# A linear-attention and bilinear-FFN kernel: shorter zero products at the start, two second-weight products side by side, one slot's transposes and loads ahead of a store

## The chip, the cores and the metric

The kernel runs on one core of a Trainium2 chip. The metric is the device time of one execution in microseconds (us). The engines are TensorE (PE for its products, PEld for its weight loads), VectorE (DVE), ScalarE (ACT), GpSimd (POOL) and SyncE (SP), which issues nearly all DMAs. The five engines run side by side and wait for each other on semaphores.

## The reference

There are two steps. The first is a linear attention with a decaying state, over 4 batches, 8 heads, 768 positions and a head size of 64; the second is a bilinear feed-forward layer on its result, laid out as 3072 tokens by 512.

```python
gamma = 1.0 - 2.0 ** (-5.0 - np.arange(H))
for t in range(S):
    state = gamma * state + einsum('bhd,bhe->bhde', k[:, :, t], v[:, :, t])
    y[:, :, t] = scale * einsum('bhd,bhde->bhe', q[:, :, t], state)
x = y.transpose(0, 2, 1, 3).reshape(3072, 512)
out = ((x @ w_a) * (x @ w_b)) @ w_out        # w_a, w_b: 512 x 1536; w_out: 1536 x 512
```

## The kernel before

**Attention.** The 3072 tokens are cut into 24 slots of 128 positions (six in each batch). The decay is folded into k and q by tables (`scaled`, L285, writes both into one bf16 tile `kqb`), so that a slot needs: the transposes of its k and q (`kqT`), the scores inside the slot (`at`, L338 and L452), a mask on DVE (`aT`), the product with the running state (`inter`), the product with v (`intra`), the update of the state (`update`), and a copy of the result to `xt`. The first six slots are taken as three pairs by functions whose names end in 2 (`casts2`, `flip2`, `scores2`, `update2`, `intra2`, `inter2`, `leave2`); `flip2` transposes on TensorE. From slot 6 on, `casts` makes `kqb` on POOL, `flip` (L311) has SP issue one DMA transpose of it, and `casts(t)` ends with the loads of slot t+2. `turn(new, old)` then does the TensorE part of a slot pair.

**Feed-forward.** `xt` is consumed in seven groups of slots (`TILES`, group J). For each of twelve column blocks ft of the weights, `ffn_a(J, ft)` (L533) makes four products that add up to a, and ACT copies them to `asb`; `ffn_g(J, ft)` (L545) makes four products with the second weight, and DVE multiplies them by `asb` into `ht` (L547). For group 0 the first two blocks are taken in two halves of the tokens: columns 0 to W2 belong to the first slot pair, W2 to 2*W2 to the second. The last product is done by `ffn_out` for group 0, and for the others by a seven-product scheme (`Group`, `Unit`, `single`). A PSUM bank for a or g comes from a ring of three (`psff`): the oldest idle bank is taken, and it is given back in program order.

**Weights.** They arrive as f32 by DMA into `wst` tiles and are cast to bf16 on POOL (`cast_w`, L244). `cast_w(0, parts=2)` makes four casts: the first weight's blocks 0 and 1 (`wa_bf`), then the second weight's blocks 0 and 1 (`wb_bf`).

**Order.** Everything is written out by hand in one program order, and `seq` chains the instructions of each engine in that order. SP is one queue: loads, DMA transposes and stores leave it in the order in which the program reaches them. A finished output tile is not stored at once: it goes to `held`, and `store()` (L559) issues what is held at the next `ffn_out(.., 0)` or `ffn_ab`.

**Zero products.** `warm(pool, tag, *cols)` (L514 to L519) gives TensorE products of a zero tile that nobody reads. The tile `zero` is f32, and in the trace each such f32 product is two TensorE instructions. There are five calls ahead of the first weights: after them in order stand the transposes of k (pair 0), those of q, the scores and the first state update, and, for pair 1, the scores. The last call takes a bank of the ring `psff` and gives it back.

**Around slot 9.** The program order there is: `ffn_out(0, 2, 0)`, which stores tile 1 of the output; `ffn_out(0, 2, 1)`; `turn(6, None, V_)`; the sums of `ht` on DVE; `ffn_out(0, 3, 0)`, which stores tile 2; `ffn_out(0, 3, 1)`; `casts(9)`; `turn(None, 6)`; `single(1, ..)`, which stores tile 3; `casts(10)`; `casts(11)`; and, after more blocks, `turn(8, None)` and `turn(10, 8)`. The scores of slot 11 are the first TensorE work of `turn(10, 8)`.

Of the kernel before, what the change touches and what calls it, by code (L numbers as in the profile page):

```python
# [29 lines left out]
def kernel(  # L30
# [10 lines left out]
    nc = tc.nc  # L41
    P = 128
    B, H, S, D = q.shape
    NCH = S // P
    HP = H // 2
# [25 lines left out]
    psat = ctx.enter_context(tc.tile_pool(name="psat", bufs=1, space=bass.MemoryType.PSUM))  # L71
# [23 lines left out]
    psff = Ring()  # L95
# [4 lines left out]
    def seq(bi):  # L100
        ins = bi.ins
        prev = last.get(ins.engine)
        if prev is not None:
            tc.add_manual_dep(ins, prev.name, nosync, reason="program order")
        last[ins.engine] = ins
        return bi
# [4 lines left out]
    def load_slot(t, names="kqv"):  # L111
        b, ci = divmod(t, NCH)
        for nm in names:
            src = {"k": k, "q": q, "v": v}[nm]
            if nm == "q":
                if t % 2 == 0:
                    load_two(nm, src, b, ci // 2, t)
                continue
            if t % 2 == 0:
                whole[nm] = raw.tile([P, 2, H, D], F32, tag=nm + "f", name=nm + "f")  # L120
            raws[nm, t] = whole[nm][:, t % 2]
            s = src[b, :, ci * P : (ci + 1) * P, :].rearrange("h p d -> p h d")
            seq(nc.sync.dma_start(out=raws[nm, t], in_=s))
# [5 lines left out]
    def load_two(nm, src, b, u, t):  # L129
        f = raw.tile([P, H, 2, D], F32, tag=nm + "f", name=nm + "f")  # L130
        s = src[b, :, 2 * u * P : 2 * (u + 1) * P, :].rearrange("h (p two) d -> p h two d", two=2)
        seq(nc.sync.dma_start(out=f, in_=s))  # L132
        for par in range(2):
            raws[nm, t + par] = f[:, :, par, :]
# [5 lines left out]
    def load_wide(nm, n):  # L140
        src = {"a": moe_w_a, "b": moe_w_b}[nm]
        for i in range(2):
            st = wstage.tile([P, 2, 2 * WC], F32, tag="w", name="wst" + nm)
            s = src[2 * i * P : 2 * (i + 1) * P, 2 * n * WC : 2 * (n + 1) * WC]
            seq(nc.sync.dma_start(out=st, in_=s.rearrange("(c p) f -> p c f", p=P)))
            wst[nm, n, i] = st
# [16 lines left out]
    def issue_loads(n):  # L163
        for _ in range(min(n, len(pending))):
            what = pending.pop(0)
            n = int(what[1:])
            if what[0] in "ab":
                load_wide(what[0], n)
            elif what[0] in "kqv":
                load_two(what[0], {"k": k, "q": q, "v": v}[what[0]], 0, n, 2 * n)  # L170
            else:
                {"p": load_pair, "s": load_slots, "t": load_slot, "w": load_w, "o": load_o}[what[0]](n)
# [5 lines left out]
    zero = osbp.tile([P, DM], F32, tag="osb", name="zero")  # L178
# [6 lines left out]
    ident = const.tile([P, P], BF16, name="ident")  # L185
# [20 lines left out]
    gbd = [const.tile([P, HP, P], BF16, name=f"gbd{i}") for i in range(2)]  # L206
# [33 lines left out]
    def cast(engine, dst, src):  # L240
        if engine is nc.scalar:
            seq(nc.scalar.copy(dst, src))
        else:
            seq(engine.tensor_copy(dst, src))  # L244
# [29 lines left out]
    def scaled(eng, t, i):  # L274
        tab = tabs[0] if i else tabs[1 if t < 2 * PAIRS else 2]
        dst, src, tab = kqb[t][:, i], raws["kq"[i], t], tab[:, t % NCH]
        if t < 2 * PAIRS:
            dst, src = (x.rearrange("p (hp r) d -> p hp r d", r=2) if x is src else x
                        for x in (dst, src))
            tab = tab.rearrange("p (hp r) o -> p hp r o", r=2).to_broadcast([P, HP, 2, D])  # L280
        else:
            dst = dst.rearrange("p hp r d -> p r hp d")
            src = src.rearrange("p (r hp) d -> p r hp d", r=2)
            tab = tab.rearrange("p (r hp) o -> p r hp o", r=2).to_broadcast([P, 2, HP, D])
        seq(eng.tensor_tensor(dst, src, tab, op=ALU.mult))  # L285

    def new_nat(t):
        kqb[t] = nat.tile([P, 2, HP, 2, D], BF16, tag="kqb", name="kqb")
        kb[t], qb[t] = kqb[t][:, 0], kqb[t][:, 1]
        vb[t] = nat.tile([P, H, D], BF16, tag="vb", name="vb")  # L290

    def casts(t):
        new_nat(t)
        scaled(nc.gpsimd, t, 0)
        scaled(nc.gpsimd, t, 1)
        if t not in range(12, 20):
            cast(nc.gpsimd, vb[t], raws["v", t])
        flip(t)
        u = t + 2
        if u in V_LATE:  # L300
            load_slot(u, "kq")
            if u % 2:
                load_slot(u - 1, "v")
                load_slot(u, "v")
        elif u < NSLOT:
            load_slot(u)

    def flip(t):
        if t % 2 == 0:
            kqT[t // 2] = tra.tile([P, 2, 2, HP, P], BF16, tag="kqT", name="kqT", bufs=3)  # L310
        seq(nc.sync.dma_start_transpose(  # L311
            out=kqT[t // 2][:, t % 2].rearrange("p a b c -> p (a b) c"),
            in_=kqb[t].rearrange("p a hp r d -> p (a hp r d)")))
# [195 lines left out]
    def xcols(J, kt, c0, c1):  # L509
        if J < 2:  # L510
            return xt[J][:, c0 // P : c1 // P, kt, :]
        return xt[J][:, kt, c0:c1]

    def warm(pool, tag, *cols):  # L514
        idle = pool.tile([P, HP * P], F32, tag=tag, name="idle")
        for n in cols:
            seq(nc.tensor.matmul(idle[:, :n], zero[:, :P], zero[:, :n], start=True, stop=True,
                                 skip_group_check=True))
        psff.back(idle)  # L519

# [18 lines left out]
    def ffn_g(J, ft, c0=0, c1=None):  # L539
        c1 = TILES[J] * P if c1 is None else c1  # L540
        fs = slice(ft * P, (ft + 1) * P)
        bank = psff.tile([P, 4 * P], F32, tag="ff", name="g")
        g = bank[:, : c1 - c0]
        for kt in range(KT):
            seq(nc.tensor.matmul(g, wb_bf[:, kt, fs], xcols(J, kt, c0, c1),  # L545
                                 start=(kt == 0), stop=(kt == KT - 1)))
        seq(nc.vector.tensor_tensor(ht[J][:, ft, c0:c1], g, asbs.pop((J, ft, c0)), op=ALU.mult))  # L547
        psff.back(bank)
# [8 lines left out]
    def store():  # L557
        for dst, src in held:
            seq(nc.sync.dma_start(out=dst, in_=src))  # L559
        held.clear()  # L560
# [3 lines left out]
    def ffn_out(J, i, n):  # L564
        if n == 0:
            store()
            plain_out[i] = psff.tile([P, DM], F32, tag="ff", name="o")
        o = plain_out[i]
        for ft in range(NP * n, NP * n + NP):
            seq(nc.tensor.matmul(o, ht[J][:, ft, i * P : (i + 1) * P], wo_bf[:, ft],  # L570
                                 start=(ft == 0), stop=(ft == NFT - 1), skip_group_check=True))
        if n:
            osb = osbp.tile([P, DM], F32, tag="osb", name="osb")
            cast(nc.scalar, osb, o)
            psff.back(o)
            held.append((rows(J, i // 2, i % 2), osb))

    def rows(J, u, r):
        n0 = (sum(TILES[:J]) + 2 * u) * P
        return out[n0 : n0 + 2 * P, :].rearrange("(n r) d -> r n d", r=2)[r]  # L580
# [36 lines left out]
    def hsums(J, a, b, eng):  # L617
        for s in (2, 1, 4):
            hsum(J, s, a, b, eng)
# [257 lines left out]

    D_, G_, A_ = nc.vector, nc.gpsimd, nc.scalar
    K, Q = 0, 1
    warm(psat, "y1", 512, 512, 256)  # L880
    casts2(0, {(K, 1): D_, (K, 0): D_, (Q, 1): D_, (Q, 0): D_})
    flip2(0, K, [((0, 1), A_)])
    warm(psat, "y1", 128)
    flip2(0, Q, [((1,), D_)])
    flip2(0, Q, [((0,), D_)])
    warm(psat, "y1", 256)
    scores2(0, 1)
    scores2(0, 0, "ff")
    update2(0, 0)
    warm(psat, "y1", 512)  # L890
    casts2(1, {(K, 0): G_, (K, 1): G_, (Q, 1): D_, (Q, 0): D_})
    update2(0, 1)
    intra2(0, 1, True)
# [2 lines left out]
    flip2(1, K, [((0, 1), A_)])  # L896
    leave2(0, (A_, A_))
    flip2(1, Q, [((1,), D_), ((0,), D_)])
    warm(psff, "ff", 256)
    scores2(1, 0, "ff")  # L900
    scores2(1, 1)
    update2(1, 0)
# [1 line left out]
    W2 = 2 * P  # L904
# [5 lines left out]
    leave2(1, (A_, D_))  # L910
    update2(1, 1)
    ffn_g(0, 0, 0, W2)
    issue_loads(100)
    cast_w(1, parts=2)
    ffn_a(0, 0, W2, 2 * W2)
    ffn_a(0, 1, W2, 2 * W2)
    ffn_g(0, 1, 0, W2)
    ffn_g(0, 0, W2, 2 * W2)
    ffn_g(0, 1, W2, 2 * W2)
    cast_wide("a", 1)  # L920
# [62 lines left out]
    turn(6, None, V_)  # L983
    hsum(1, 3, 0, 6)
    hsums(1, 0, 6, V_)
    ffn_out(0, 3, 0)
    ffn_out(0, 3, 1)
    casts(9)
    turn(None, 6)
    single(1, AT0, AT1, FF)  # L990
    casts(10)
# [100 lines left out]
```

## Time and profile before

| | |
|---|---|
| time, median of 3 runs | 219.66 us (219.35 to 219.67) |
| the profiled execution | 219.63 us |
| its span, first to last instruction | 217.9 us |
| TensorE busy | 211.4 us, 97% of the span |
| VectorE, ScalarE, GpSimd busy | 65%, 46%, 68% |
| granted TensorE clock over the span | 1.000 |
| read from and written to HBM | 28.31 MB and 6.29 MB |

The profiled execution's own time, its span and what lies around it, is 0.03 us under the median of the runs. In the profile a line "start, us, engine, line, operation, out<-in, xcount" is a run of like instructions: when the first began and how long it was until the last ended. "SPq" is the time in which SP issued a DMA. "[0.29 <-POOL wb_bf L244]" says how long the engine sat idle just before, and what it waited for.

### The profile page before, as it was taken

How to read it: one execution, taken by the hardware profiler on the slowest of the kernel's cores; microseconds unless marked ns; L12 is line 12 of the kernel's file. 1: busy time of each engine (PE TensorE's matmuls, PEld its weight loads, DVE VectorE, ACT ScalarE, POOL GpSimd, SP SyncE). 2: the span in 40 equal slices, each digit the busy share in tenths (PEclk: the TensorE clock that was granted, in tenths of full speed). 3: DMA queues.
4: the chain of work that ended last, by engine and by line, in shares of the span. 5: the costliest groups of instructions: out<-in, count | busy, mean ns of one | idle time of the engine just before them, and what ended most of it. 6: DMA issues, size and time to landing. Idle time of an engine off the chain costs nothing.

```text
span 217.9 us, 5672 instructions
## 1 busy us (share of the span) xinstructions
PE 211.4 (97%) x2244; PEld 143.6 (66%) x2244; DVE 141.5 (65%) x258; ACT 100.8 (46%) x221; POOL 147.9 (68%) x172
## 2 busy tenths in 40 slices
PE   7889999999999999999999999999999999999994
PEld 3557445587458888888888665456864444458883
DVE  3776446845873486355477245896687797688962
ACT  3256335343224444455576344455546656652331
POOL 5265876779344578579856948899999999960000
PEclk9999999999999999999999999999999999999999
DMA  6999999999999999999999996990022000000055
GB/s 163 290 321 365 384 303 361 384 263 236 181 239 257 196 231 214 195 232 245 196 202 272 207 193 173 237 150 3 5 86 106 0 2 3 0 2 0 27 193 169
DMA packets 85146, 39.68 MB, mean 182 GB/s; under 512 B 57472, under 2 KB 78848, under 8 KB 85120
## 3 DMA queue, kind: packets, MB, share of 16 engines
q1 hardware_dynamic: 84976, 39.26, 80.7%
q8 instruction: 17, 0.28, 0.6%
q14 instruction: 9, 0.07, 0.1%
q10 hardware_dynamic: 144, 0.07, 0.1%
HBM read 28.31 MB, written 6.29 MB: 159 GB/s over the span
## 4 chain that ended last, share of the span: by engine, by line
PE 84%; SPq 7%; DMA 6%; issue 1%; POOL 0%; ACT 0%; DVE 0%; ACTq 0%
PE g L545 17%; PE a L533 17%; PE mA L650 11%; PE uA L801 10%; PE mB L650 6%; PE uB L801 5%; PE o L570 5%; SPq L132 4%; DMA wstb<-in_moe_w_b_dram 4%; PE mC L650 3%; DMA kqT<-kqb 2%; PE uC L801 2%; PE at L338 2%; PE y L386 2%; PE st L356 1%; PE y L376 1%
## 5 line engine op out<-in xcount | busy, mean ns | idle before, releaser
L547 DVE TENSOR_TENSOR ht<-g,asb 128x256 bf16<-128x256 f32 (+1 forms) x74 | 37.2, 503 | 37.5 <-PE g L545 34.5
L545 PE MATMUL g<-xt,wb_bf 128*128 128x256 bf16 (+1 forms) x296 | 52.5, 304 | 0.3 <-POOL wb_bf L244 0.3
L533 PE MATMUL a<-xt,wa_bf 128*128 128x256 bf16 (+1 forms) x296 | 52.7, 304 | 0.1
L536 ACT CAST asb<-a 128x256 bf16<-128x256 f32 (+1 forms) x74 | 32.3, 437 | 39.2 <-PE a L533 37.7
L545 PEld LDWEIGHTS <-wb_bf 128*128 128x128 bf16 x296 | 28.6, 98 | 12.8 <-POOL wb_bf L244 0.4
L533 PEld LDWEIGHTS <-wa_bf 128*128 128x128 bf16 x296 | 28.1, 98 | 12.2 <-POOL wa_bf L244 0.4
L285 POOL TENSOR_TENSOR kqb<-kf,ktab 128x512 bf16<-128x512 f32 x22 | 23.0, 1050 | 16.8 <-DMA kf<-in_k_dram 13.4
L808 ACT COPY snap<-uA 128x512 f32<-128x512 f32 x36 | 20.0, 588 | 15.5 <-PE uA L801 15.4
L650 PEld LDWEIGHTS <-hs 128*128 128x128 bf16 x234 | 22.8, 98 | 4.0
L285 POOL TENSOR_TENSOR kqb<-qf,qtab 128x512 bf16<-128x512 f32 x18 | 19.0, 1054 | 7.1 <-DMA qf<-in_q_dram 7.1
L344 DVE TENSOR_TENSOR aT<-at,mask 128x512 bf16<-128x512 f32 x36 | 22.3, 682 | 0.3
L657 ACT COPY snaps<-mA 128x256 f32<-128x256 f32 x30 | 11.0, 374 | 20.1 <-PE mA L650 20.1
L650 PEld LDWEIGHTS <-ht 128*128 128x128 bf16 x180 | 17.5, 98 | 3.3
L583 POOL TENSOR_TENSOR hs<-ht,hs 128x384 bf16<-128x384 bf16 (+1 forms) x17 | 16.8, 993 | 2.8 <-DVE ht L547 2.6
L583 POOL TENSOR_TENSOR hs<-ht 128x384 bf16<-128x384 bf16 (+2 forms) x12 | 13.8, 1154 | 3.0 <-DVE ht L547 3.0
L583 POOL TENSOR_TENSOR ht<-gsb,asb 128x512 bf16<-128x512 bf16 x13 | 15.1, 1173 | 1.1 <-DVE gsb L583 1.1
L650 PE MATMUL mA<-wsum,hs 128*128 128x256 bf16 x120 | 15.2, 273 | 0.0
L244 POOL CAST vb<-vf 128x512 bf16<-128x512 f32 x16 | 9.9, 630 | 7.5 <-DMA vf<-in_v_dram 7.4
L583 DVE TENSOR_TENSOR osb<-mB,snaps 128x256 f32<-128x256 f32 x20 | 8.4, 422 | 8.6 <-PE mB L650 4.8
L583 DVE TENSOR_TENSOR asb<-uB,snap 128x512 bf16<-128x512 f32 x12 | 8.2, 684 | 3.9 <-ACT snap L808 1.8
L570 PE MATMUL o<-wo_bf,ht 128*128 128x512 bf16 x48 | 10.7, 379 | 0.0
L397 ACT CAST xt<-y 128x512 bf16<-128x512 f32 x18 | 9.7, 589 | 0.6 <-PE y L386 0.4
(101 smaller groups left out, 333.4 us busy)
## 6 DMA issues: line engine op xcount, KB each, us to landing
qf<-in_q_dram SPq DMA_DIRECT2D x12, 512.0 KB, 6.5
out_dram<-osb SPq DMA_DIRECT2D x21, 256.0 KB, 4.2
kf<-in_k_dram SPq DMA_DIRECT2D x18, 256.0 KB, 4.6
vf<-in_v_dram SPq DMA_DIRECT2D x18, 256.0 KB, 5.2
wsta<-in_moe_w_a_dram SPq DMA_DIRECT2D x6, 512.0 KB, 7.9
wstb<-in_moe_w_b_dram SPq DMA_DIRECT2D x6, 512.0 KB, 8.2
wsto<-in_moe_w_out_dram SPq DMA_DIRECT2D x6, 512.0 KB, 8.7
kf<-in_k_dram SPq DMA_DIRECT2D x3, 512.0 KB, 7.3
```

Source lines behind the costliest of these rows:

```text
L285: seq(eng.tensor_tensor(dst, src, tab, op=ALU.mult))
L344: seq(nc.vector.tensor_tensor(aT[t][:, r], at[r], mask.to_broadcast([P, HP, P]), op=ALU.mult))
L533: seq(nc.tensor.matmul(a, wa_bf[:, kt, fs], xcols(J, kt, c0, c1), start=(kt == 0), stop=(kt == KT - 1)))
L536: seq(nc.scalar.copy(asb, a))
L545: seq(nc.tensor.matmul(g, wb_bf[:, kt, fs], xcols(J, kt, c0, c1), start=(kt == 0), stop=(kt == KT - 1)))
L547: seq(nc.vector.tensor_tensor(ht[J][:, ft, c0:c1], g, asbs.pop((J, ft, c0)), op=ALU.mult))
L570: seq(nc.tensor.matmul(o, ht[J][:, ft, i * P : (i + 1) * P], wo_bf[:, ft], start=(ft == 0), stop=(ft == NFT - 1), skip_group_check=True))
L583: seq(eng.tensor_tensor(dst, x, y, op=op))
L650: seq(nc.tensor.matmul(m, w, right[:, j], start=(first and j == 0), stop=(j == NP - 1), skip_group_check=True))
L657: seq(nc.scalar.copy(self.snaps[:, n], self.bank["A"]))
L801: seq(nc.tensor.matmul(m, w, right[:, k], start=(first and k == 0), stop=(k == 1), skip_group_check=True))
L808: seq(nc.scalar.copy(self.snaps[n], self.bank["A"]))
```

## The change

- `warm` takes 0 as a size: it then makes one bf16 product, with the identity as the stationary tile and the still empty state tile `gbd[0]` (128 x 512 bf16) as the moving one.
- The first call loses its product of 256 columns; the call with 128 columns goes; the call with 256 columns ahead of the first scores and the one with 512 columns behind the first state update become one bf16 product each; the call with 256 columns ahead of pair 1's scores goes, and with it its turn in the ring `psff`.
- `ffn_g(0, 1, 0, W2)` moves from behind the two `ffn_a` of the second half to right behind `ffn_g(0, 0, 0, W2)`.
- `casts(9)` moves from behind `ffn_out(0, 3, 1)` to ahead of `ffn_out(0, 3, 0)`. On POOL nothing else stands between the two places; on SP, slot 9's transpose and the loads of slot 11's k and v now come before the store of output tile 2, which then stands next to the store of tile 3.

```diff
     def warm(pool, tag, *cols):
         idle = pool.tile([P, HP * P], F32, tag=tag, name="idle")
         for n in cols:
-            seq(nc.tensor.matmul(idle[:, :n], zero[:, :P], zero[:, :n], start=True, stop=True,
+            lhs, rhs = (zero[:, :P], zero[:, :n]) if n else (ident, gbd[0].rearrange("p a b -> p (a b)"))
+            seq(nc.tensor.matmul(idle[:, : n or HP * P], lhs, rhs, start=True, stop=True,
                                  skip_group_check=True))
         psff.back(idle)
...
-    warm(psat, "y1", 512, 512, 256)
+    warm(psat, "y1", 512, 512)
     casts2(0, {(K, 1): D_, (K, 0): D_, (Q, 1): D_, (Q, 0): D_})
     flip2(0, K, [((0, 1), A_)])
-    warm(psat, "y1", 128)
     flip2(0, Q, [((1,), D_)])
     flip2(0, Q, [((0,), D_)])
-    warm(psat, "y1", 256)
+    warm(psat, "y1", 0)
     scores2(0, 1)
     scores2(0, 0, "ff")
     update2(0, 0)
-    warm(psat, "y1", 512)
+    warm(psat, "y1", 0)
     casts2(1, {(K, 0): G_, (K, 1): G_, (Q, 1): D_, (Q, 0): D_})
...
     flip2(1, Q, [((1,), D_), ((0,), D_)])
-    warm(psff, "ff", 256)
     scores2(1, 0, "ff")
     scores2(1, 1)
...
     ffn_g(0, 0, 0, W2)
+    ffn_g(0, 1, 0, W2)
     issue_loads(100)
     cast_w(1, parts=2)
     ffn_a(0, 0, W2, 2 * W2)
     ffn_a(0, 1, W2, 2 * W2)
-    ffn_g(0, 1, 0, W2)
     ffn_g(0, 0, W2, 2 * W2)
     ffn_g(0, 1, W2, 2 * W2)
...
     hsums(1, 0, 6, V_)
+    casts(9)
     ffn_out(0, 3, 0)
     ffn_out(0, 3, 1)
-    casts(9)
     turn(None, 6)
```

## The prediction

> **What bounds the kernel now.** I read the page first, then TensorE's waits, then the chain of work that ended last, and last the timeline of the two places that the chain names.
>
> ```profile
> span 217.9 us, 5672 instructions
> PE 211.4 (97%) x2244; PEld 143.6 (66%) x2244; DVE 141.5 (65%) x258; ACT 100.8 (46%) x221; POOL 147.9 (68%) x172
> ...
> PE 84%; SPq 7%; DMA 6%; issue 1%; POOL 0%; ACT 0%; DVE 0%; ACTq 0%
> ...
> PE tp L442 <- DVE kqb L285: 0.9, 3, 0.4
> PE idle L517 <- ACT kqT L242: 0.4, 1, 0.4
> PE g L545 <- POOL wb_bf L244: 0.3, 1, 0.3
> ...
> 10.37 8.20 DMA wstb<-in_moe_w_b_dram
> 18.63 0.62 POOL wb_bf L244
> 19.30 0.61 PE g L545 x4
> ...
> 73.05 2.23 SPq L132
> ...
> 75.81 5.22 DMA kqT<-kqb
> 81.08 0.64 PE at L338 x32
> ...
> 1.50:5.95 4.45, 4.43 (x6) 1.85 (x6) 1.83 (x11) 1.29 (x4) 2.08 (x9) 1.00 0.90 233
> ...
> 19.30:81.00 61.70, 61.70 (x602) 41.40 (x602) 37.44 (x69) 23.92 (x55) 40.69 (x48) 1.00 1.13 281
> ```
>
> The chain is TensorE's for 84% of the span, and what is not TensorE's lies in two places. Up to 19.30 the path is the load of the second weight (issued at 10.37, landed 8.20 later), then its cast on POOL, then the first g. From 19.30 TensorE is never idle for long: the table by stage counts 61.70 us busy of 61.70 up to 81. (A busy TensorE in these records can still hide a short wait, since ends of products are modelled.) At 81.08 the chain leaves TensorE once more: slot 11's scores start when its DMA transpose lands (75.81 + 5.22 = 81.03). From there on the chain is TensorE's to the end. So an edit counts if it moves the g at 19.30, if it adds TensorE time or a wait behind it, or if it moves the landing at 81.03.
>
> **The zero products.**
>
> ```profile
> 1.52 4.63 PE L517 MATMUL idle<-zero 128*128 128x512 f32 x6 [1.52 <-DVE zero L179]
> 6.55 0.62 PE L442 MATMUL tp<-ident,kqb 128*128 128x128 bf16 x8 [0.40 <-DVE kqb L285]
> 7.01 0.44 PE L517 MATMUL idle<-zero 128*128 128x128 f32 x2
> 8.57 0.65 PE L517 MATMUL idle<-zero 128*128 128x256 f32 x2
> 10.36 1.13 PE L517 MATMUL idle<-zero 128*128 128x512 f32 x2
> 14.72 0.70 PE L517 MATMUL idle<-zero 128*128 128x256 f32 x2 [0.42 <-ACT kqT L242]
> 15.35 0.64 PE L452 MATMUL at<-kqT 64*64 64x128 bf16 x32
> 25.38 3.62 PE L533 MATMUL a<-xt,wa_bf 128*128 128x512 bf16 x16
> ...
> 13.88 0.88 DVE L244 COPY kqT<-tp 128x512 bf16<-128x512 bf16 x2
> 16.33 0.33 PEld L533 LDWEIGHTS <-wa_bf 128*128 128x128 bf16 x4 [0.21 <-POOL wa_bf L244]
> 18.59 0.42 PE L473 MATMUL st<-vb,kqb 64*64 64x64 bf16 x16
> ```
>
> The first burst is 4.63 us for 512+512+256 columns, each in two instructions, so 2560 columns at 1.8 ns. Without the 256 it has 2048 columns: 3.7 us, 0.9 less. The call of 128 takes 0.44. A bf16 product of 512 columns is priced by the row of sixteen such products, 3.62/16 = 0.23 us; put in for 0.65 and for 1.13 it saves 0.42 and 0.90. The last call takes 0.70. In all 0.9 + 0.44 + 0.42 + 0.90 + 0.70 = 3.4 us of TensorE time goes, every bit of it ahead of 19.30.
>
> What it brings there: behind the first burst TensorE waited 0.40 us for `kqb` and will now wait 1.3. The transposes of q wait for DVE's `kqb` as before (three waits, 0.9 us in all, with the one ahead of k's). Ahead of pair 1's scores the gain is real: DVE's copies of `kqT` end at 13.88 + 0.88 = 14.76, so the scores can start near 14.85 instead of 15.35. But the a behind them wait for POOL's `wa_bf` at 16.33, and from there to 18.59 + 0.42 = 19.01 follow products that no edit touches. TensorE then waits for `wb_bf`, 0.3 us by the waits, and this wait absorbs what is left. I book **0** for the zero products. The cover is the load of the second weight; if it were gone, that wait is what there would be to win. The bank that the last call took from the ring `psff` only turns the ring by one: the scores take the two oldest of three idle banks instead of the two youngest, which is never later.
>
> [...] The products run at two rates: 1.8 ns a column in the first burst, but the later rows of 512 and of 256 differ by 2 x 256 = 512 columns and by 1.13 - 0.65 = 0.48 us, 0.9 ns a column, half as much, though the table by stage gives a granted clock of 1.00 for the burst (1.50 to 5.95) as for all that follows. So TensorE started at half rate and was at full rate by 6.55, about 5 us after it began. The burst that did this shrinks from 4.6 to 3.7 us, and the gap behind it grows from 0.4 to 1.3 us.
>
> [...]
>
> **The two g.**
>
> ```profile
> 18.63 1.17 POOL L244 CAST wb_bf<-wstb 128x512 bf16<-128x512 f32 x2 [1.79 <-DMA wstb<-in_moe_w_b_dram]
> 18.83 0.69 DVE L244 CAST xt<-y 128x512 bf16<-128x512 f32 x1 [0.54 <-PE y L496]
> 19.75 0.93 PE L533 MATMUL a<-xt,wa_bf 128*128 128x256 bf16 x7
> ```
>
> No instruction is added. The second g needs the second cast of `wb_bf`, which ends at 18.63 + 1.17 = 19.80; the first g started 0.05 behind its own cast (18.63 + 0.62 = 19.25), so the second can start at 19.85. The slot that it is moved into opens at 19.75, where the a now starts. So TensorE waits about **0.1 us** more there. In the other direction nothing is gained as long as the first g waits for POOL: the a that came in between needs the second half of `xt`, which DVE finishes at 18.83 + 0.69 = 19.52, and had it. Behind the moved g are queued all later TensorE products; ACT and DVE wait for those in turn, and the banks they free come round later by the same 0.1. The bound below is 0 (the second cast is quicker, or the first g later), above 0.15.
>
> **Slot 9 and slot 11.**
>
> ```profile
> 79.99 0.60 PE L533 MATMUL a<-xt,wa_bf 128*128 128x256 bf16 x4
> 80.42 0.60 PE L545 MATMUL g<-xt,wb_bf 128*128 128x256 bf16 x4
> ...
> 64.64 1.57 SPq L559 DMA_DIRECT2D out_dram<-osb  x2
> 66.30 1.55 SPq L311 DMA_TRANSPOSE kqT<-kqb  x1
> 67.90 1.14 SPq L123 DMA_DIRECT2D kf<-in_k_dram  x1
> ...
> 69.97 0.80 SPq L559 DMA_DIRECT2D out_dram<-osb  x1
> ```
>
> The moved step issues work on POOL (two products into `kqb`, one cast) and on SP (one transpose, two loads). On POOL no other instruction stands between the two places, so nothing changes. On SP the step is moved past one store only: of the two at 64.64 the first belongs to the call of `ffn_out` before. So slot 9's transpose and slot 11's loads leave earlier by half of 1.57, about 0.8 us, and the store leaves behind them at about 69, beside the one of 69.97.
>
> Who is waiting for that? TensorE's beat at 79.99 and 80.42 is 0.43 us for four products, so the scores of slot 11 could have begun at 80.86 and began at 81.08: **0.22 us** is all that this place holds. Their transpose is issued at 75.81, behind slot 10's transpose and a load of q that SP was issuing until 73.05 + 2.23 = 75.28. All the bytes that went ahead of it before go ahead of it now, so its landing is bounded by 81.03 (queue unchanged) and by 0.8 us less (the store drains beside other things). Below 80.9 it no longer matters. I take a landing a few tenths earlier, near 80.7: the transposes are what everybody waits for in this queue, and one of them is no longer stuck behind two stores in a row.
>
> **The sum.** Without the landing TensorE would reach the scores of slot 11 at 80.86 + 0.1 = 80.96; the landing at 80.7 is then not late. So they start 0.1 us earlier than at 81.08, and TensorE carries that to the end. The profiled execution took 219.63 us, 0.03 under the median: 219.63 - 0.1 = 219.5. If the landing does not move, the 0.1 of the second g vanishes in the wait that was there anyway, and the time is 219.6. I forecast **219.55 us**. About 0.2%, 0.44 us, is what a measurement of this kernel can tell from no change, so this is "no change"; its own range is 219.3 to 219.9.
>
> **Rivals.**
>
> ```profile
> q8 instruction: 17, 0.28, 0.6%
> ...
> q8 instruction: 1, 0.02, 3.5%
> wsta<-in_moe_w_a_dram SPq DMA_DIRECT2D x1, 512.0 KB, 7.0
> wstb<-in_moe_w_b_dram SPq DMA_DIRECT2D x1, 512.0 KB, 8.2
> ```
>
> *A, the second weight lands earlier, faster.* The load of the second weight, 8.2 us, took 1.2 longer than that of the first, 7.0, though both are 512 KB. Instructions come by DMA too, in 17 transfers of 16 KB, and one of them falls between 15 and 17 us, just when this load is due. TensorE has most instructions (2244 products and as many weight loads), so the transfer is likely its own; six products and their weight loads fewer by then shift it to a later point of the program. If it then misses the load, `wb_bf` is ready over 1 us sooner, the first g starts behind the products that end at 19.01 (overlapped by the usual 0.2, so near 18.85), and both g fill the time until `xt` is there at 19.52. That is 0.45 us; with the 0.22 at slot 11, if its transpose also comes that much earlier, up to 0.67: 219.0 to 219.2. Against it: six products are 0.1 us where they stand as dense as at 15.35 (32 in 0.64 us), far less than the load's lateness. Chance 0.22.
>
> *B, the queue, slower.* The store now stands beside another one, right ahead of slot 10's transpose. If that transpose waits for both to land, slot 10's loads and slot 11's transpose slip behind it, by up to one store, 0.8 us; the scores of slot 11 then start at 81.8, and the time is up to 220.3. It decides from a landing later than 80.9. For it: the transpose at 75.81 took 5.22 us in a crowded queue. Against it: bytes and order ahead of slot 10 are the same in sum. Chance 0.08.
>
> *C, half rate, slower.* If the shorter burst leaves TensorE at half rate, the delays up to 16.3 are partly absorbed by the 0.5 us won ahead of pair 1's scores; but the products from 16.33 to 19.01, 2.7 us at full rate, would take 5.4, and the first g would come near 21.5: 2.2 us late, 221.7, and more if the half rate lasts into the g. It decides if the half rate lasts beyond some 16 us; up to 13 us it would cost nothing, since the path is the load's. Between 6.55 and 16 TensorE is busy most of the time. Chance 0.08.
>
> **How the numbers follow.** No change as summed: 0.60; A 0.22; B 0.08; C 0.08; 0.02 for something else. The range reaches down through A to 218.95 and up through most of B to 220.2, and leaves out C. Faster by over 0.2%: 0.20 from A and 0.03 from the edge of the first case, 0.23. Slower by over 0.2%: C, half of B and the rest, 0.14. Within: 0.63.
>
> **What would show it.** In the profile after, right would be: the load of the second weight still 8.2 us, the first g near 19.3 waiting for POOL, the second g near 19.85, the a behind it near 20.3; slot 9's transpose about 0.8 us earlier; no wait at slot 11's scores, which start near 80.96. A first g near 18.85 with a shorter load is A; scores of slot 11 behind 81.1 with a wait for their transpose is B; transposes and scores between 6.55 and 16 that take twice as long are C. I am wrong on the cover if the first g moves at all, and wrong on the queue if slot 11's scores wait for anything.

## The result: slower by 1.7 us at the median, and scattered

The kernel before: 219.43 us (median of 22 runs, 219.13 to 219.94). The changed kernel: **221.16 us** (22 runs, 219.38 to 223.34); the ratio is 1.0064, 95% interval 1.0044 to 1.0084. The ratio leaves out three runs of the changed kernel that lie over 1.5% above its fastest one (the ratios of e2 and e9 below leave out two and one), so it understates the loss; medians and counts here are over all runs.

The scatter says as much as the median. The 22 runs of the kernel before span 0.8 us. Of the changed kernel four lie at 219.38 to 219.69, where the forecast was, five at 220.42 to 220.79, eight at 221.09 to 221.72 and five at 222.43 to 223.34. So the change costs nothing in some runs and up to 3.9 us in others.

### The profile page after: what moved, and what is told of

Its sections match the earlier page's. It is cut to its first block, busy times and chain, and to the rows that moved or that the text cites. A ratio compares the mean times of both kernels' runs of the same rounds, so it can differ in the third digit from the quotient of the medians.

```text
span 219.6 us, 5656 instructions
## 1 busy us (share of the span) xinstructions
PE 212.3 (97%) x2236; PEld 145.1 (66%) x2236; DVE 141.1 (64%) x258; ACT 100.7 (46%) x221; POOL 148.6 (68%) x172
## 4 chain that ended last, share of the span: by engine, by line
PE 93%; DMA 3%; DVE 2%; ACT 0%; issue 0%; SPq 0%; DVEq 0%
PE g L546 19%; PE a L534 19%; PE mA L651 12%; PE uA L802 9%; PE mB L651 6%; PE o L571 5%; PE uB L802 5%; PE mC L651 3%; DMA qf<-in_q_dram 3%; PE at L338 2%; PE uC L802 2%; PE y L386 2%; PE st L356 2%; PE tp L442 2%; PE st L473 1%; DVE aT L458 1%
## 5 line engine op out<-in xcount | busy, mean ns | idle before, releaser
L534 PE MATMUL a<-xt,wa_bf 128*128 128x256 bf16 (+1 forms) x296 | 52.6, 304 | 0.0
L546 PE MATMUL g<-xt,wb_bf 128*128 128x256 bf16 (+1 forms) x296 | 52.5, 304 | 0.0
L546 PEld LDWEIGHTS <-wb_bf 128*128 128x128 bf16 x296 | 28.6, 98 | 12.5
L534 PEld LDWEIGHTS <-wa_bf 128*128 128x128 bf16 x296 | 28.1, 98 | 11.8 <-DVE xt L244 0.3
```

The lines of the kernel that those rows point to most:

```text
L534: seq(nc.tensor.matmul(a, wa_bf[:, kt, fs], xcols(J, kt, c0, c1), start=(kt == 0), stop=(kt == KT - 1)))
```

## The profile after

The profiled execution of the changed kernel took 221.32 us, 1.69 more than that of the kernel before (219.63). First the page (span, engines, chain), then TensorE's waits (us in total, times, the longest). Lines of the kernel behind `warm` count one higher than before (L517 is L518, L533 is L534, L545 is L546).

```profile
span 219.6 us, 5656 instructions
PE 212.3 (97%) x2236; PEld 145.1 (66%) x2236; DVE 141.1 (64%) x258; ACT 100.7 (46%) x221; POOL 148.6 (68%) x172
...
PE 93%; DMA 3%; DVE 2%; ACT 0%; issue 0%; SPq 0%; DVEq 0%
...
PE tp L442 <- DVE kqb L285: 1.6, 2, 1.5
PE at L452 <- DVE kqT L244: 0.5, 1, 0.5
PE st L473 <- ACT gbd L478: 0.3, 1, 0.3
```

TensorE has eight products fewer and is busy 0.9 us longer (212.3 against 211.4): the same work took more time. Its share of the chain rose from 84% to 93%, and the first g's wait for POOL's `wb_bf` is gone from the waits. TensorE itself is now what is late. The timeline of its first 23 us (start, duration, instruction, count) shows where, with POOL's cast of the second weight below:

```profile
1.52 3.78 PE L518 MATMUL idle<-zero 128*128 128x512 f32 x4 [1.52 <-DVE zero L179]
6.75 1.03 PE L442 MATMUL tp<-ident,kqb 128*128 128x128 bf16 x8 [1.45 <-DVE kqb L285]
9.70 1.07 PE L452 MATMUL at<-kqT 64*64 64x128 bf16 x32
10.70 1.03 PE L473 MATMUL st<-vb,kqb 64*128 64x128 bf16 x8
15.20 1.89 PE L442 MATMUL tp<-ident,kqb 128*128 128x128 bf16 x16
17.60 0.64 PE L452 MATMUL at<-kqT 64*64 64x128 bf16 x32 [0.51 <-DVE kqT L244]
21.19 1.05 PE L546 MATMUL g<-xt,wb_bf 128*128 128x256 bf16 x8
...
17.39 1.17 POOL L244 CAST wb_bf<-wstb 128x512 bf16<-128x512 f32 x2 [0.33 <-DMA wstb<-in_moe_w_b_dram]
```

Eight transposes took 1.03 us; before they took 0.62. The 32 products of a call of scores took 1.07 at 9.70 and 0.64 at 17.60, with the same shapes: TensorE ran at half rate until about 17 us. It reached pair 1's scores at 17.60 instead of 15.35 and the first g at 21.19 instead of 19.30, 1.89 late, although `wb_bf` was ready at 17.39 + 1.17 = 18.56. At slot 11, the last place where the chain used to leave TensorE, nothing is waited for, and 82.84 against 81.08 is still 1.8 late:

```profile
82.31 0.60 PE L546 MATMUL g<-xt,wb_bf 128*128 128x256 bf16 x4
82.84 0.73 PE L338 MATMUL at<-kqT 64*64 64x128 bf16 x32
```

So rival C came, nearly at its price (first g "near 21.5", 221.7 us). What had to be settled: is it the shorter burst alone, as C had it, or also the products taken out behind it; do they act by their number, their kind or their time; and do the two moves do what was forecast?

## Experiments

Every kernel ran beside the kernel before on the same chip, whose medians there were 219.41, 219.41 and 219.36. Over all sets 3 of its 119 runs lie above 220.2, so the share of runs above 220.2 is a sharp mark; such a run is called lost here. "Up to 9 us" counts the zero products of the first burst / between k's and q's transposes / ahead of the first scores; a "b" is a bf16 product of 512 columns, all else is float32 columns.

| kernel | up to 9 us | behind | both moves | median us | ratio, 95% | above 220.2 |
|---|---|---|---|---|---|---|
| before | 512,512,256 / 128 / 256 | 512, 256 | no | 219.41 | | 3 of 119 |
| changed | 512,512 / – / b | b | yes | 221.16 | 1.0044–1.0084 | 18 of 22 |
| e1 | 512,512,256 / – / b | b | yes | 219.54 | 1.0004–1.0048 | 5 of 12 |
| e2 | 512,512 / 128 / 256 | 512, 256 | no | 220.3 | 1.0010–1.0053 | 7 of 12 |
| e3 | as before | as before | yes | 219.35 | 0.9985–1.0008 | 0 of 12 |
| e4 | 512,512,b,b / – / b | b | yes | 220.18 | 1.0015–1.0064 | 6 of 12 |
| e5 | 512,512,b,b / b / b,b | b,b,b,b; b,b | yes | 219.46 | 0.9997–1.0014 | 0 of 11 |
| e6 | 512,512,256 / 128 / b | b | yes | 219.38 | 0.9983–1.0012 | 0 of 11 |
| e7 | none | none | yes | 221.20 | 1.0067–1.0095 | 4 of 4 |
| e8 | as before | 512 | yes | 219.44 | 0.9991–1.0009 | 0 of 11 |
| e9 | 512,512 / 128 / b | b | yes | 219.53 | 0.9997–1.0028 | 2 of 12 |
| e10 | 512,512,256 / 4 transposes / b | b | yes | 219.51 | 0.9997–1.0028 | 1 of 12 |
| e11 | 512,512,512 / – / b | b | yes | 219.40 | 0.9990–1.0007 | 0 of 11 |
| e12 | 512,512,256 / 128 / – | – | yes | 219.63 | 1.0003–1.0056 | 4 of 12 |

### e3: the two moves alone

The kernel before with `ffn_g(0, 1, 0, W2)` and `casts(9)` moved as in the change, all zero products as before.

```diff
     ffn_g(0, 0, 0, W2)
+    ffn_g(0, 1, 0, W2)
...
-    ffn_g(0, 1, 0, W2)
...
+    casts(9)
     ffn_out(0, 3, 0)
     ffn_out(0, 3, 1)
-    casts(9)
```

> The two moves alone (second g behind the first, slot 9 ahead of the store), with all zero products of the kernel before. If the loss is the rate's: 219.3 to 219.5 us, as forecast (second g near 19.85, no wait at slot 11's scores, which start near 80.96 where they started at 81.08). If a move costs: above 220.4, with a wait of over 1 us at one of the two places.

Measured 219.35 us, ratio 0.9996 (0.9985 to 1.0008), none of 12 above 220.2. Its timeline:

```profile
19.18 1.17 PE L545 MATMUL g<-xt,wb_bf 128*128 128x256 bf16 x8 [0.25 <-POOL wb_bf L244]
20.18 1.04 PE L533 MATMUL a<-xt,wa_bf 128*128 128x256 bf16 x8
...
80.43 0.60 PE L545 MATMUL g<-xt,wb_bf 128*128 128x256 bf16 x4
80.96 0.73 PE L338 MATMUL at<-kqT 64*64 64x128 bf16 x32
...
18.51 1.17 POOL L244 CAST wb_bf<-wstb 128x512 bf16<-128x512 f32 x2 [1.76 <-DMA wstb<-in_moe_w_b_dram]
```

The two g together take 1.17 us; in the changed kernel, where both casts were long ready, the same eight took 1.05. The difference, 0.12, fits the wait that was forecast as 0.1: the second cast ends at 18.51 + 1.17 = 19.68, and the four products of the first g need 0.43 from 19.18 on. The scores of slot 11 start at 80.96, as forecast, with no wait for their transpose. So the moves do what they say, and the loss is not theirs.

### e1 and e2: one half of the zero products each

e1 is the changed kernel with the first burst as it was; e2 is the kernel before with the first burst shortened and nothing else changed.

```diff
 e1, against the changed kernel
-    warm(psat, "y1", 512, 512)
+    warm(psat, "y1", 512, 512, 256)
 e2, against the kernel before
-    warm(psat, "y1", 512, 512, 256)
+    warm(psat, "y1", 512, 512)
```

> The changed kernel with one thing put back: the product of 256 columns in the first burst (0.9 us of TensorE, so the burst is 4.4 us again). Theory F, the length of the first burst decides when TensorE leaves its half rate: 219.4 us in all runs, first g near 19.3 or earlier, transposes at 6.55 at 56 ns each. Theory M, the products taken out between 7 and 15 us decide (the chain of transposes, scores and updates is too thin without them): still 221 us with runs scattered between 219.4 and 223. If both matter: the median near 220, scattered.

> The kernel before with one thing taken away: the product of 256 columns in the first burst; all other zero products and the old order stay. Theory F: 221 us in the median, scattered between 219.4 and 223 as the changed kernel is. Theory M: 219.4 us in all runs, since the products from 7 to 15 us are still there. If both matter: between, near 220.

Both are in between: 5 of 12 runs above 220.2 for e1, 7 of 12 for e2. Neither half is the whole cause. Their profiles show two different failures. e1's table by stage (start:end, length, busy time and count of TensorE, weight loads, DVE, ACT, POOL, then the granted clock):

```profile
2.25:5.66 3.41, 3.41 (x6) 1.35 (x4) 1.01 (x3) 0.55 (x3) 1.40 (x6) 1.00 1.05 275
5.66:9.07 3.41, 1.94 (x19) 1.06 (x18) 2.76 (x6) 1.01 (x1) 0.42 (x1) 1.00 1.22 290
9.07:12.49 3.42, 3.04 (x46) 2.27 (x46) 2.69 (x6) 0.73 (x2) 2.69 (x4) 0.50 1.22 290
12.49:15.90 3.41, 3.41 (x54) 2.67 (x52) 1.25 (x2) 0.91 (x3) 1.60 (x4) 0.50 1.12 331
15.90:19.31 3.41, 2.79 (x83) 2.30 (x82) 2.69 (x6) 3.17 (x7) 2.01 (x4) 1.00 1.09 353
```

The rate did rise, at 5.66 (eight transposes in 0.62 us at 6.44). But TensorE was busy for only 1.94 of the next 3.41 us, and at 9.07 the clock fell to 0.50 and stayed there for two such stretches, to 15.90. (The 1.00 of the first row is no measurement: the record of the clock begins with the first rise, and the burst ran at half rate, as the prediction read from its durations.) The profiled run took 221.06 us.

e2's timeline shows the other failure, a late rise:

```profile
6.45 1.03 PE L442 MATMUL tp<-ident,kqb 128*128 128x128 bf16 x8 [1.14 <-DVE kqb L285]
9.76 1.00 PE L452 MATMUL at<-kqT 64*64 64x128 bf16 x32
10.69 0.62 PE L473 MATMUL st<-vb,kqb 64*128 64x128 bf16 x8
...
16.22 0.64 PE L452 MATMUL at<-kqT 64*64 64x128 bf16 x32
...
19.81 0.61 PE L545 MATMUL g<-xt,wb_bf 128*128 128x256 bf16 x4
```

Here the transposes still run at half rate (1.03 us for eight), and the full rate begins at 10.55, by the record of the clock. Then it lasts.

The mean granted clock of every run, not only of the profiled one, tells the two failures apart: since the record shows 1.00 up to the first rise, a mean of 0.992 or less is a fall behind it. All five lost runs of e1 have 0.976 or 0.984, so the rate fell in each. Of e2's seven, four have 0.977 to 0.992 and three have 1.000, a late rise alone. Of the changed kernel's 18, twelve have 0.967 to 0.984 and six 1.000 (one of these is the profiled run, whose record is empty). All five of its runs at 220.42 to 220.79 have 0.984: over a span of 218.7 us that is 7.0 us at half rate, two stretches of 3.41.

In the three profiles where the rate falls and rises again, its changes lie whole steps of 3.41 us apart: at 5.66, 9.07 and 15.90 in e1 (one step and two), at 5.10, 8.51 and 18.75 in e4 (one and three), at 4.65, 11.47 and 14.89 in e12 (two and one; both below). I take it from these three that the rate is set anew every 3.41 us. The steps do not begin at one place of the kernel: the first rise came at 6.59 in the profile of the kernel before, at 7.29 in e3, at 5.66 in e1, at 4.65 in e6 (below). Counted back from it in steps of 3.41, the first boundary lies anywhere from 0.31 us (e2) to 3.18 us (before) behind the first instruction, over the 13 profiles that have a record. Boundaries that fall differently in each run would also explain how one program takes 219.38 us in one run and 223.34 in the next; no two profiles of one program show it here.

### e4 and e5: kind or time

e4 is the changed kernel with two bf16 products added to the first burst; e5 gives back, in bf16 products, all the time that the change took out.

```diff
 e4
-    warm(psat, "y1", 512, 512)
+    warm(psat, "y1", 512, 512, 0, 0)
 e5: as e4, and
+    warm(psat, "y1", 0)          # between k's and q's transposes
-    warm(psat, "y1", 0)          # ahead of the first scores
+    warm(psat, "y1", 0, 0)
-    warm(psat, "y1", 0)          # behind the first update
+    warm(psat, "y1", 0, 0, 0, 0)
+    warm(psff, "ff", 0, 0)       # ahead of pair 1's scores
```

> The changed kernel with two bf16 products of 512 columns added to the first burst, about 0.43 us each at half rate, so as long as the f32 product of 256 that was taken out, in two instructions as well. Theory F by time: as e1_burst_back, 219.4 us. If only f32 products of two passes count for the rate: as the changed kernel, 221 us scattered. Theory M: 221 us scattered, as e1_burst_back.

> The changed kernel with every zero product that the change removed or halved given back in time, but as bf16 products of 512 columns (two take about the time of one float32 product of 256 columns at the same rate): the first burst 512, 512 and two bf16 ones, one bf16 between k's and q's transposes, two before the first scores, four after the first update, two before pair 1's scores; both moves kept. If only TensorE's busy time keeps the rate (theory): median 219.35 as with the moves alone, at most 1 run of 12 above 220.2, the first g near 19.2. If the products must be float32 ones, or many columns in one instruction (rival): scattered like the changed kernel, median 220 to 221.2, half of the runs above 220.2.

e5: 219.46 us, none of 11 above 220.2. The time that was taken out can be given back in another kind of product, so these products need not be float32. e4 behaves like e1 (6 of 12), and its table by stage shows the same fall, one stretch after the rise:

```profile
1.69:5.10 3.41, 3.41 (x5) 1.16 (x6) 0.99 (x4) 1.10 (x4) 1.89 (x8) 1.00 0.89 235
5.10:8.51 3.41, 1.68 (x17) 0.84 (x16) 2.71 (x5) 1.01 (x1) 0.00 (x0) 1.00 1.22 290
8.51:18.75 10.24, 9.33 (x154) 7.21 (x154) 5.84 (x12) 3.45 (x7) 6.71 (x10) 0.50 1.15 320
18.75:22.16 3.41, 3.41 (x79) 2.77 (x74) 2.67 (x6) 2.34 (x7) 1.83 (x4) 1.00 1.06 381
```

Busy 1.68 of 3.41, then half rate for three stretches, 10.24 us.

### e6, e9, e11: which of them, and where

All three are the changed kernel with other zero products up to 9 us:

```diff
-    warm(psat, "y1", 512, 512)
+    warm(psat, "y1", 512, 512, 256)   # e6;  e9: 512, 512;  e11: 512, 512, 512
     casts2(0, {(K, 1): D_, (K, 0): D_, (Q, 1): D_, (Q, 0): D_})
     flip2(0, K, [((0, 1), A_)])
+    warm(psat, "y1", 128)             # e6 and e9;  not in e11
```

> The changed kernel with the first burst's third product (256 columns) and the 128 columns between k's and q's transposes given back; the calls before the first scores, after the first update and before pair 1's scores stay as changed. If the hole between the two groups of transposes (near 6.9 to 8.5) is what lets the rate fall after its first rise: median 219.4 to 219.5, 0 to 2 runs of 12 above 220.2. If the later calls that the change shortened or removed carry the rate as well (rival): like the kernel with the first burst alone given back, median 219.5 to 220.2, about 5 of 12 above 220.2.

> The changed kernel with only the 128 columns between k's and q's transposes given back; the first burst stays at 512, 512. With the burst's 256 alone 5 of 12 runs lay above 220.2, with both 0 of 11, with neither 18 of 22. If each of the two does its own part (the burst for the rise of the rate, the 128 against its fall): between neither and the burst alone, 5 to 8 of 11 above 220.2, median 220.2 to 221. If the 128 alone carries it (rival): at most 2 of 11 above 220.2, median 219.4.

> The changed kernel with a longer first burst, 512, 512, 512, and nothing between k's and q's transposes, so that the idle time ahead of the first transposes goes too. If the hole between the groups of transposes (about 0.5 us without work, in 6.9 to 7.6) is the cause by itself: still 3 to 6 of 11 above 220.2. If it is the busy share of the whole 3.41 us that holds that hole, wherever in it the work lies (rival): at most 2 of 11 above 220.2, median 219.4 to 219.5, with the first transposes at most 0.3 later than 6.45.

e6: none of 11 above 220.2, 219.38 us. Two float32 products, 256 and 128 columns, are enough to undo the whole loss (221.16 to 219.38). With the rate full, its pair 1 scores start at 14.74, where the prediction had 14.85.

e9 missed what the theory expected of it (5 to 8 of 11): 2 of 12 and 219.53 us, the rival's number. The 128 columns alone bring nearly as much back as both calls do. Why e2, which has the same burst and the same 128 columns and more behind them, did worse with 7 of 12, I can't show; a zero product at half rate also takes longer (the 256 columns at 8.66 in e2 took 1.17 us, in the kernel before 0.65), and 12 runs are few. By their clocks e9's two lost runs are falls (0.967 and 0.977), and none of its 12 is a late rise, where e2 had three.

e11 decides between the two readings of the fall. The hole between the groups of transposes is as wide as in e1 (0.59 us waited there), yet none of 11 runs is above 220.2. The stretches behind the first rise, e11 first, then e6 and e9:

```profile
5.20:8.61 3.41, 2.42 (x20) 1.09 (x18) 2.74 (x5) 1.01 (x1) 0.01 (x1) 1.00 1.22 290
...
4.65:8.06 3.41, 2.11 (x17) 1.12 (x15) 2.44 (x4) 0.93 (x1) 0.00 (x0) 1.00 1.22 290
...
5.46:8.87 3.41, 1.84 (x19) 1.22 (x20) 2.74 (x6) 1.01 (x1) 0.12 (x1) 1.00 1.22 291
```

The work may lie ahead of the hole (e11) or in it (e6); what went with the rate here is how much of it falls into the 3.41 us. The rate held behind 2.42 and 2.11, and fell behind 1.94 (e1) and 1.68 (e4). e9 is the exception: it held behind 1.84. The busy time of these records (whose ends are modelled) puts the border near 2.0 of 3.41, and not sharply: with 1.84 held in e9 and 1.94 fallen in e1, it can't be exactly what is counted.

### e10 and e12: transposes, and the products behind

e10 is e6 with four transposes that nothing reads in place of the 128 columns; e12 is e6 without the two bf16 products that the change leaves.

```diff
 e10
-    warm(psat, "y1", 128)
+    for hp in range(HP):
+        seq(nc.tensor.transpose(spare[:, 0, hp, :], ..., ident))
 e12
-    warm(psat, "y1", 0)     # ahead of the first scores, and behind the first update
```

> The kernel with the burst and the 128 columns given back, but the 128 columns (0.44 us of a zero product) replaced by four more transposes of 128 columns (0.40 us), which nothing reads. If a transpose counts as work for the rate (theory one, as the busy share alone would have it): as with the 128 columns, 0 to 1 of 11 above 220.2, median 219.4. If it does not count (theory two): as with the burst alone given back, 3 to 6 of 11 above 220.2, by 1.1 to 2 us each.

> The kernel before's first burst (512, 512, 256) and its 128 columns between the transposes, and no other zero product; both moves kept. If by 9 us the kernel's own products hold the rate (theory): 219.3 to 219.45, at most 1 of 11 above 220.2. If the two short products of 512 columns that the change leaves (0.38 us each at full rate, near 8.5 and 10.3) are needed too (rival): 3 or more of 11 above 220.2, by one step of 3.41 us at half rate, 1 to 1.7 us.

e10: 1 of 12 above 220.2, within what was expected if transposes count, but one run away from nothing and four from e1: a lean, not a proof. The tables by stage lean the same way: without its transposes (1.41 us) the stretch of 1.84 that held in e9 has 0.43 us of work left, while e12's stretch of 1.84 that fell (below; 0.45 of transposes) has 1.39. e12: the theory said that the kernel's own products hold the rate by 9 us. It fell: 4 of 12 above 220.2, 219.63 us, and e12's table by stage shows the step (the last line is e6's, for the same place):

```profile
4.65:8.06 3.41, 2.06 (x17) 1.12 (x15) 2.38 (x4) 0.87 (x1) 0.00 (x0) 1.00 1.22 290
8.06:11.47 3.41, 1.84 (x49) 1.45 (x49) 2.74 (x6) 0.87 (x3) 2.00 (x3) 1.00 1.22 290
11.47:14.89 3.42, 3.42 (x56) 2.69 (x54) 2.20 (x4) 0.81 (x3) 1.95 (x4) 0.50 1.16 314
...
8.06:11.48 3.42, 2.40 (x51) 1.76 (x52) 2.75 (x7) 0.81 (x3) 2.07 (x3) 1.00 1.22 290
```

2.06 held, 1.84 did not. In e6, whose profile has its first rise at the same 4.65, the stretch from 8.06 to 11.48 holds 2.40: the short product near 8.5 and the one near 10.3 carry it. The count above 220.2 understates this. By their clocks (0.975 to 0.992) the rate fell in nine of e12's 12 runs, and in five of them the time stayed at 219.44 to 219.79: one stretch at half rate at that place is nearly hidden (in the profile, 0.992 and 219.69 us, the first g starts at 19.55). In e3, e5, e6, e8 and e11 no run is below 0.998.

### e7 and e8: the two ends

e7 is the changed kernel without any zero product, e8 the kernel before with both moves and without its last call (256 columns ahead of pair 1's scores).

```diff
 e7
-    warm(psat, "y1", 512, 512)
-    warm(psat, "y1", 0)      # both
 e8, against the kernel before
-    warm(psff, "ff", 256)
```

> The changed kernel without any zero product, both moves kept. If TensorE's busy share in the first 17 us sets when its full rate begins (theory): the full rate begins later than in the changed kernel, in most runs beyond 17 us, the first g at 21.5 or later, median 222 to 224. If the products that are left in the changed kernel do nothing (rival): 221.2, as the changed kernel.

> The kernel before with both moves, without the zero product of 256 columns ahead of pair 1's scores, all other zero products kept. If by then (near 14.8) the rate no longer depends on it: 219.3 to 219.4, at most 1 run of 12 above 220.2, the first g where it was, since the load of the second weight ends last there. If that call still carries the rate (rival): 2 or more of 12 above 220.2, by one step of 3.41 us at half rate, 1 to 1.7 us.

e7 took 221.06 to 221.28 us in four runs: the rival's number (221.2), not the theory's (222 to 224). Its full rate begins at 16.21, by the record of the clock, in time for pair 1's scores, and the first g comes at 20.81:

```profile
6.52 1.03 PE L442 MATMUL tp<-ident,kqb 128*128 128x128 bf16 x8 [6.52 <-DVE kqb L285]
17.22 0.64 PE L452 MATMUL at<-kqT 64*64 64x128 bf16 x32 [0.62 <-DVE kqT L244]
20.81 1.05 PE L546 MATMUL g<-xt,wb_bf 128*128 128x256 bf16 x8
```

So at the median the zero products that the change leaves in buy nothing: 221.16 with them, 221.20 without any. The four runs without any lie within 0.22 us of each other, while the 22 of the changed kernel spread over 3.96; four runs are too few to settle why. e8 is 219.44 with none of 11 above 220.2: the last call isn't needed for the rate, and leaving it out gains nothing either, since the second weight still ends last.

No version beats the kernel before: the best medians (e3 219.35, e6 219.38, e11 219.40) lie within the intervals of no change.

## Why the prediction was wrong

- **The failed step: "I book 0 for the zero products. The cover is the load of the second weight."** The cover hid the time of these 3.4 us, and hid it well (e6 and e8 lose nothing by what they leave out). It could not hide what they do for the rate of everything behind them. The term measured 1.7 us at the median, 0 to 3.9 by run.
- **Rival C was the mechanism, and 0.08 was its mis-sized chance.** The prediction read the half rate correctly from the durations, and the burst and the gap came as worked out (3.78 us, then 1.45 of waiting, against 3.7 and 1.3). The sentence that made C unlikely was "Between 6.55 and 16 TensorE is busy most of the time". That was read from the kernel before, with its zero products. Without them the stretch behind an early rise held 1.68 (e4) to 1.94 us (e1) of work in 3.41, and the rate fell. And where the rise was late, being busy did not bring it soon: in the profile of the changed kernel TensorE is busy, at half rate, for 9.6 of the 10.2 us from 6.75 to 16.98, and the rate is full only from about then. The share should have been worked out for the changed program, and its rate with it.
- **C was also incomplete.** It knew only a late rise. In e1, e4 and e12 the rate rises and falls again; in e1 it fell at 9.07, without a long wait: the longest between 5.66 and 9.07 was 0.57 us.
- **The place of decision was half right.** Half rate beyond some 16 us did cost: it lasted to about 17 in the profile of the changed kernel, and the first g moved to 21.19; "I am wrong on the cover if the first g moves at all" was the right test. But "up to 13 us it would cost nothing" does not hold: in e2's profile the rate is full from 10.55 on, and still pair 1's scores start at 16.22 (15.35 before), the first g at 19.81 (19.30 before), and the run took 220.32 us.
- **The two moves: right in the result,** by e3: 0.12 us more for the two g, 80.96 for slot 11's scores, no wait there, and a sum that can't be told from nothing. That 80.96 came to the digit is luck. Where nothing is waited for, the scores start 0.53 us behind the last g (80.43 to 80.96 in e3, 82.31 to 82.84 in the changed kernel), not 0.43, so the place held 0.13 us and not 0.22; and e3's first g started 0.12 earlier than in the kernel before, with its cast (18.51 against 18.63), which hid the 0.12 of the second g. In the queue the move did more than was booked: slot 9's transpose was issued at 63.59 instead of 66.30, 2.7 us earlier and not 0.8, and slot 11's at 73.49 instead of 75.81; it took 5.7 us, so it landed near 79.2 and not near 80.7. Rival B's wait appears in one of the twelve profiles that have the moves (e1, 0.46 us at 82.69).
- **Rival A's first half came, for another reason.** The second weight was ready early in the changed kernel (the cast at 17.39 instead of 18.63) and in e1, e2, e4 and e7 (17.06 to 17.26). But it was not early in e6 (18.46) and e12 (18.65), which also have fewer instructions than the kernel before. It is early where pair 1's scores start at 16.22 (e2) or later, and not where they start at 15.96 (e12) or sooner. So the number of instructions does not do it (the change takes out eight products, not the six of the prediction). What goes with it in all 14 profiles is A's own condition, the transfer of instructions: it starts at 15.70 to 16.40 us in the nine where the weight is late, and at 16.78 to 17.75 in the five where it is early. That TensorE's lateness is what moves this transfer is argued from that order, not shown by an experiment. It won nothing, since TensorE came later than the weight.

## What to carry to other kernels

Before a filler product is booked at nothing because its time is hidden, ask what it does for the rate of what follows, and work out TensorE's busy share of the **changed** program in every stretch of 3.41 us: where it came near 2 us here, the rate fell in some profiles (1.84 in e12, 1.94 in e1) and held in others (1.84 in e9, 2.00 in e5). Look at the spread of the runs beside the median, and at the granted clock of each run; one lucky profile (four of 22 runs here) would have shown no loss. To win the time back, put the work into the stretch that is thin: here 256 and 128 columns were enough, and a burst longer by 512 columns did as well.

## What the runs showed of the hardware

- The granted clock moved in steps of 3.41 us between 0.50 and 1.00 (e1, e4, e12), and fell back after a single stretch with 1.68 (e4), 1.84 (e12) or 1.94 us (e1) of work, with no wait above 0.57 us in e1. It held behind 2.00 (e5), 2.06 (e12), 2.11 (e6), 2.12 (e8), 2.15 (e10) and 2.42 (e11), and once behind 1.84 (e9).
- The way up did not go by the busy time of the records: at half rate TensorE was busy for 3.04 of 3.41 us in e1 (9.07 to 12.49) and the rate did not rise, while it rose behind 2.86 in e5 (0.97 to 4.38); in e4 it was busy for 9.33 of 10.24 us before it rose. The same first burst of 3.78 us was enough in e9 (rise at 5.46) and not in e2 (10.55). What exactly is counted stays open.
- The record of the granted clock shows 1.00 up to the first rise (in e2 from 3.72 to 10.55), although the durations show half rate there; the profile of the changed kernel has no clock row at all. The rate had to be read from equal shapes: 1.03 (e2) against 0.62 us (before) for eight transposes.
- The load of the second weight (512 KB) was followed by its cast at 17.06 to 17.39 us where the next transfer of instructions (16 KB) started at 16.78 or later (17.75 in the changed kernel, cast at 17.39), and at 18.46 to 18.65 where it started at 16.40 or sooner (15.94 in the kernel before, cast at 18.63), in 14 of 14 profiles.
